# Dynamic convolution and two MoE layers: the first ten cells in an order written out by hand, with the weight units in pairs one cell ahead

## The chip, the core and the metric

The kernel runs on one NeuronCore of a Trainium2 chip. The metric is the device time of one execution in microseconds (us), the median of several runs. The engines are TensorE (PE in the views; its weight loads are PEld), VectorE (DVE), ScalarE (ACT), GpSimd (POOL) and SyncE (SP, which here issues nearly all DMAs). Nothing waits for another core.

## What is computed

A dynamic convolution over the sequence (a softmax over seven taps for each token and head, and the weighted sum of the seven last tokens), then two MoE layers that share one shape: 8192 tokens of 192 features, 2048 hidden features.

```python
def _attn_ref(x, weight_gen):
    B, S, D = x.shape                      # 2, 4096, 192
    H, K = (weight_gen.shape[2], weight_gen.shape[3])   # 8, 7
    w = np.exp(weight_gen - np.max(weight_gen, axis=-1, keepdims=True))
    w = w / (np.sum(w, axis=-1, keepdims=True) + 1e-09)
    x_pad = np.concatenate([np.zeros((B, K - 1, D), dtype=np.float32), x], axis=1)
    idx = np.arange(S)[:, None] + np.arange(K)[None, :]
    x_unf = x_pad[:, idx, :].reshape(B, S, K, H, D // H)
    return np.einsum('bshk,bskhg->bshg', w, x_unf).reshape(B, S, D)

def _moe_ref(x, w_in, w_out):              # layer 0
    h = x @ w_in
    g = np.where(h > 0.0, h, np.exp(np.minimum(h, 0.0)) - 1.0)
    return g @ w_out

def _moe2_ref(x, w_in, w_out):             # layer 1
    h = x @ w_in
    return (h * np.clip(h + 3.0, 0.0, 6.0) / 6.0) @ w_out
```

All of it is float32.

## The kernel before

**Tiling.** The 8192 tokens are 16 blocks of 512. A block goes through a layer in eight *cells*, one for each 256 hidden features, so there are 16 x 2 x 8 = 256 cells, numbered n; the first eight are block 0 in layer 0. The main loop runs over n. In cell n TensorE makes the first product of cell n (x times w_in, into two PSUM banks `h`, one for each half k of the features, from the list `hset`, whose pair alternates with n) and the second product of cell n-3 (g times w_out, summed over the eight cells of a block in the banks `acca` and `accb`; LAG is 3). Both use only 64 of the 128 rows at a time, so matmuls go in pairs, one of each half. Cells 0 to 2 have no second product.

**Precision.** Each float32 operand is split in a high and a low part (`xh`, `xl`; `wi_h`, `wi_l`; `gh`, `gl`), and a product is three: high times high, low times high, high times low. `first_product` lists nine matmuls for each half: "hl1", say, is the high part of w with the low part of x for piece 1.

**A cell's other work.** `act_a` (ScalarE, two passes L520, L521 for each half) and `gate` (VectorE, L537) make r, the activation of h; `round_g` (ScalarE, L527) casts r to gh; `rest_g` (VectorE, L531) makes gl.

**Weight units.** The weights of layer 0 are split on the chip while the first cells run: sixteen units, i0 to i7 (a cell's part of w_in) and o0 to o7 (w_out). A unit goes through: the raw load by DMA (`load_w`; four raw buffers, RAWS; three DMAs for an i unit and one for an o unit); `begin`, an Abs on ScalarE (L147); s0, s1, s2 on VectorE (L151, L154, L158); the cast of the high part on ScalarE (L168); s3, s4 on VectorE (L166, L175); `p5`, three matmuls on TensorE (L180 to L182); and `p6`, the cast of the low part on ScalarE (L187). Before, the groups are [i0], [i1 o0], [i2 o1] and so on, and group n+1 gets its p5 behind the matmuls of cell n, in the banks `aux` and `acca` (and `accb` once), and its p6 behind that cell's activations. A `Stream` deals out the other steps at the end of each cell by due times.

**Queues.** From cell 2 on a DMA that is asked for goes to the list `waiting`, and `transfers` issues a few whenever a half's last matmul in `accb` is done (`told`); up to cell 7 that is two DMAs for the first half and three for the second.

**Block 0's input.** Its convolution is done by VectorE and GpSimd, two tokens of each four. `prepare(0, 0)` transposes it on TensorE into the banks of hset[0], ScalarE casts xh (L328), VectorE subtracts for xl (L330), and then each half of the partitions needs the other's rows as well: four DMAs on SP (two for xh, two for xl), 64x768 each. `Stream`, `round_g`, `rest_g` and `wst.run` set where each step stands in its engine's queue, since every engine works in program order.

Of the kernel before, what the change touches and what calls it, by code (L numbers as in the profile page):

```python
# [17 lines left out]
def kernel(  # L18
# [67 lines left out]
    boot = cpool.tile([P, NF * 2 * D], F32R, tag="wo1", name="boot")  # L86
    w_in = [w.bitcast(U32) for w in (w_in1, w_in2)]
# [25 lines left out]
    class Unit:  # L113


        def __init__(self, kind, m, q):
            self.kind, self.m, self.q = kind, m, q
            self.raw = load_w(kind, m, q)
            self.hw, self.lw = self.raw[:, :, 1], self.raw[:, :, 0]

# [11 lines left out]

        def begin(self):

            bank = aux
            if self.m == 0:

                bank = ((aux, accb), (acca[1], acca[0]))[self.kind == "o"][self.n == 2]
            self.b = bank[:, 0:UN].bitcast(U32)
            if self.m == 0:  # L140
                self.ps = bank[:, 0:UN]
                self.f = fts[self.n][:, self.u * UN:(self.u + 1) * UN].bitcast(U32)
                if self.n > 3:
# [17 lines left out]
        def s3(self):  # L161
            if self.m == 0 and self.n < 4:
                self.r = self.b
            else:
                self.r = stage.tile([P, UN], U32, tag="tr", name="tr", bufs=2)
            nc.vector.tensor_scalar(self.r, self.f, 0xFF800000, None, op0=ALU.bitwise_and)  # L166
            hi, _, v = self.parts()
            nc.scalar.copy(hi, v(self.f.bitcast(F32)))  # L168

        def s4(self):  # L170
            f = o = self.r.bitcast(F32)
            if self.m == 0:
# [51 lines left out]
    def attention(i):  # L224
# [26 lines left out]
        if i == 0:  # L251

            pw = hset[1][0][:, 0:hn * K].rearrange("p (a k) -> p a k", k=K)
            po = hset[0][0][:, 0:2 * D].rearrange("p (t e) -> p t e", e=D)
            hs = [(nc.vector, slice(0, 2), pw, po), (nc.gpsimd, slice(2, 4), w3[:, hn:, :], tmp[:, 0:2])]
        else:
            hs = [(nc.gpsimd, slice(0, TM), w3, tmp)]
# [9 lines left out]
        def product(k):  # L267
            def s():
                for eng, t, w, o in hs:
# [10 lines left out]
        def add():  # L280
            for eng, t, _, o in hs:
                eng.tensor_tensor(y[:, t, :], y[:, t, :], o, op=ALU.add)
# [18 lines left out]
        for k in range(K - 2, -1, -1):  # L301
            steps += [product(k)] + ([add] if k else [add_a, add_d])
# [6 lines left out]
    def prepare(m, i):  # L309
# [26 lines left out]
    def fold_b(m, i):  # L336
# [6 lines left out]
        nc.scalar.copy(b, accb)  # L343
# [70 lines left out]

    def first_product(n, k):
# [7 lines left out]
        for j, (w, x, s) in enumerate((  # L423
                "hh0", "hl0", "lh0", "hh1", "hl1", "lh1", "hh2", "hl2", "lh2")):
# [12 lines left out]
    def second_product(n, k, bank):  # L437
# [4 lines left out]
        acc, p, W = (acca[order.index((m, i)) % 2], accb)[bank], half[k], WO[m]  # L442
        ops = []
        for g in gg[n]:
            for c in range(2):
                for e in ([P] if bank else [0, D + HP] if g is gg[n][0] else [0]):
                    ops.append([acc, W[p, 2 * q + c, e:e + P], g[p, c], False, False, None, None])

# [7 lines left out]
    def whole_second_product(n):  # L456
# [4 lines left out]
        for bank, acc in enumerate((accb, acca[order.index((m, i)) % 2])):  # L461
# [11 lines left out]
    def matmuls(n):  # L473
# [17 lines left out]
        plan = [  # L491
            (s + j, k, op)
            for k, runs in enumerate((
                [(0, b0), (4, a0), (10, l0)], [(0, l1), (7, b1), (11, x1), (13, a1)]))
            for s, ops in runs for j, op in enumerate(ops)]
        seen = [added.pop(i) for i in range(3, NB) if n == prep[0, i] - 1]
        for _, k, (o, w, r, st, sp, wait, tell) in sorted(plan, key=lambda e: e[:2]):
# [5 lines left out]
            if tell:  # L503
# [55 lines left out]
    def later(n, out, in_):  # L559

        if now is None or now >= len(cells) or now < 2 and n == 0:
# [33 lines left out]
    units = [(k, 0, q - (k == "o")) for q in range(NQ + 1) for k in "io" if 0 <= q - (k == "o") < NQ]  # L595
    groups = [units[:1]] + [units[n:n + 2] for n in range(1, len(units), 2)]
    wtasks = [[0, n - 2, len(g)] for n, g in enumerate(groups)]
    for n in range(2 * NQ):
        c = NQ * (n + 2) if n < NB - 2 else start2 + (NQ if n % 2 else 0)
        groups.append([("io"[n % 2], 1, n // 2)])  # L600
        wtasks.append([c - 3 - 2 * (n == NB - 1), c + (3 if n < NB - 1 else 0), 1])
    made, fts = {}, {}

    def want(n):
        if n < len(groups) and n not in made:
            made[n] = [Unit(*u) for u in groups[n]]
            for u, unit in enumerate(made[n]):
                unit.n, unit.u = n, u

    def w_steps(n):  # L610
        def step(k, u):
            def s():
                if k < 0:
                    if u == 0:
                        want(n)
                        want(n + 1)
                        if groups[n][0][1] == 0:

                            fts[n] = act.tile([P, XN], F32, tag="z", name="f", bufs=2)
                    made[n][u].begin()  # L620
                else:
                    getattr(made[n][u], f"s{k}")()
            return s
        return [step(k, u) for k in range(-1, WS if groups[n][0][1] else 5) for u in range(len(groups[n]))]

    wtasks = [
        [b, d, ((WS if groups[n][0][1] else 5) + 1) * c, (lambda n: lambda: w_steps(n))(n)] for n, (b, d, c) in enumerate(wtasks) if n > 1]
    begin = {i: max(7, prep[0, i - 1]) for i in range(2, NB)}
    loads = {max(0, begin[i] - 8): i for i in begin}
# [3 lines left out]
    with tc.manual_schedule():  # L633
        nc.vector.memset(three, 3.0)
        nc.scalar.activation(warm, three, AF.Exp)
        blk[0] = load_block(0, lambda: want(0))
# [4 lines left out]
        blk[1] = load_block(1)  # L641

        todo = {"w": w_steps(0), "a": attention(0)}
        for k in "aaaawwawawawaw":
            todo[k].pop(0)()
        for s in todo["a"] + todo["w"]:
            s()
        made[0][0].p5()
        made[0][0].p6()
# [95 lines left out]
```

## Time and profile before

| | us |
|---|---|
| median of 3 runs | 1226.46 (1225.88 to 1227.32) |
| the profiled execution's own time | 1225.81 |
| its span in the trace | 1224.0 |
| PE busy | 1191.2 (97%) |
| DVE busy | 934.0 (76%) |
| ACT busy | 854.5 (70%) |
| POOL busy | 419.7 (34%) |
| chain that ended last, on PE | 92% |

The span is what the trace covers; 1.8 us of the profiled execution lie around it. The page cuts the span into 40 slices of 30.6 us, so that the ten cells this case is about (22 to about 104 us) are slices 1 to 4. Those are read from the time lines of each engine, which list every instruction with its start, its duration, and in brackets how long the engine had been idle and for whom.

### The profile page before, as it was taken

The page shows a single profiled execution, that of the slowest core. Times are in us where ns is not written, and L with a number is a line of the kernel's source. Part 1 is how long each engine was busy: PE and PEld are TensorE (multiplying, and loading weights), DVE is VectorE, ACT ScalarE, POOL GpSimd, SP SyncE. Part 2 cuts the span into 40 slices and gives each one's busy share as a digit, 9 for nine tenths or more (in the row PEclk, how much of TensorE's full clock was granted, in tenths as well). Part 3 has the DMA queues.
Part 4 walks back from the last instruction along what each step waited for, and adds up shares of the span by engine and source line. Part 5 has one row for each costly group of instructions (what it writes and reads, how often), then busy time and mean ns, then how long its engine had stood idle before and what let it go on. Part 6 is the DMA issues. An engine that isn't in the chain of part 4 may idle for free.

```text
span 1224.0 us, 25360 instructions
## 1 busy us (share of the span) xinstructions
PE 1191.2 (97%) x10146; PEld 948.3 (77%) x10146; DVE 934.0 (76%) x1222; ACT 854.5 (70%) x1337; POOL 419.7 (34%) x235
## 2 busy tenths in 40 slices
PE   3899999999999999999999999999999999999998
PEld 2568778777778777778788888888888888888887
DVE  6778999999999999998777666666666666666664
ACT  2677788888888888888886656556665555666554
POOL 8428778777778877777000000000000000000000
PEclk9899999999999999999999999999999999999999
DMA  6431122221122222111211111111101111110110
GB/s 175 126 115 62 28 88 89 89 89 61 42 76 88 89 89 72 48 59 52 61 57 52 33 34 52 52 40 53 50 23 47 53 53 40 53 36 30 53 40 27
DMA packets 33574, 75.81 MB, mean 62 GB/s; under 512 B 4404, under 2 KB 17074, under 8 KB 33456
## 3 DMA queue, kind: packets, MB, share of 16 engines
q1 hardware_dynamic: 33312, 74.00, 20.9%
q8 instruction: 80, 1.31, 0.5%
q14 instruction: 38, 0.31, 0.1%
q10 hardware_dynamic: 144, 0.20, 0.0%
HBM read 36.43 MB, written 12.58 MB: 40 GB/s over the span
## 4 chain that ended last, share of the span: by engine, by line
PE 92%; DVE 3%; ACT 3%; issue 1%; POOL 1%; DMA 0%; DVEq 0%; POOLq 0%
PE h L498 42%; PE acca L498 28%; PE accb L498 19%; DVE gl L531 1%; ACT gh L527 1%; ACT r L520 0%; PE acca L318 0%; ACT r L521 0%; PE acca L400 0%; DVE r L537 0%; DVE f L158 0%; PE acca L465 0%; ACT f L147 0%; ACT wi_h L168 0%; PE accb L465 0%
## 5 line engine op out<-in xcount | busy, mean ns | idle before, releaser
L498 PE MATMUL h<-xh,wi_l 64*128 64x512 f32 x1536 | 573.1, 397 | 3.5 <-ACT wi_l L187 3.5
L498 PE MATMUL h<-xh,wi_h 64*128 64x512 f32 x1536 | 567.5, 396 | 3.2 <-DVE xl L330 2.6
L498 PE MATMUL h<-xl,wi_h 64*128 64x512 f32 x1536 | 565.0, 395 | 0.8 <-DMA xl<-xl 0.8
L498 PE MATMUL acca<-gh,wo 64*128 64x512 f32 x2024 | 554.8, 393 | 0.0
L531 DVE TENSOR_TENSOR gl<-r,gh 128x1024 fp32r<-128x1024 f32 x256 | 395.5, 1545 | 62.2 <-ACT gh L527 61.2
L498 PEld LDWEIGHTS acca<-gh,wo 64*128 64x128 f32 x2024 | 374.1, 185 | 45.9
L523 ACT ACTIVATE r<-h,three 128x512 f32<-128x512 f32 x256 | 176.1, 688 | 222.5 <-PE h L498 113.2
L498 PE MATMUL accb<-gh,wo 64*128 64x512 f32 x1012 | 320.4, 396 | 0.0
L498 PE MATMUL accb<-gl,wo 64*128 64x512 f32 x1012 | 317.8, 393 | 0.3 <-DVE gl L531 0.3
L498 PE MATMUL acca<-gl,wo 64*128 64x512 f32 x1012 | 317.5, 393 | 0.0
L498 PEld LDWEIGHTS h<-xh,wi_l 64*128 64x128 f32 x1536 | 285.2, 186 | 40.4 <-ACT wi_l L187 5.3
L498 PEld LDWEIGHTS h<-xh,wi_h 64*128 64x128 f32 x1536 | 285.1, 186 | 39.7 <-DVE xl L330 2.8
L498 PEld LDWEIGHTS h<-xl,wi_h 64*128 64x128 f32 x1536 | 284.8, 186 | 36.6 <-DMA xl<-xl 1.4
L540 DVE SCALAR_TENSOR_TENSOR r<-r,h 128x512 f32<-128x512 f32 x256 | 175.9, 687 | 161.0 <-ACT r L523 160.2
L527 ACT CAST gh<-r 128x1024 fp32r<-128x1024 f32 x256 | 266.8, 1042 | 13.4 <-DVE r L537 12.6
L498 PEld LDWEIGHTS acca<-gl,wo 64*128 64x128 f32 x1012 | 187.2, 185 | 23.6
L498 PEld LDWEIGHTS accb<-gl,wo 64*128 64x128 f32 x1012 | 187.0, 185 | 23.6 <-DVE gl L531 0.8
L537 DVE SCALAR_TENSOR_TENSOR r<-r,h 128x512 f32<-128x512 f32 x256 | 172.8, 676 | 39.2 <-ACT r L521 37.8
L498 PEld LDWEIGHTS accb<-gh,wo 64*128 64x128 f32 x1012 | 184.8, 185 | 21.7 <-issue 1.3
L275 POOL TENSOR_TENSOR tmp<-xt,wt 128x768 f32<-128x768 f32 (+1 forms) x96 | 191.0, 1989 | 6.3
L520 ACT ACTIVATE r<-h 128x512 f32<-128x512 f32 x256 | 152.3, 595 | 48.2 <-PE acca L498 28.7
L521 ACT ACTIVATE r<-r 128x512 f32<-128x512 f32 x256 | 162.0, 633 | 8.1
(137 smaller groups left out, 751.5 us busy)
## 6 DMA issues: line engine op xcount, KB each, us to landing
xt<-in_x_dram SPq DMA_DIRECT2D x14, 960.0 KB, 6.0
xh<-xh SPq DMA_DIRECT2D x64, 192.0 KB, 2.7
xl<-xl SPq DMA_DIRECT2D x64, 192.0 KB, 2.8
raw<-in_moe_w_out_dram SPq DMA_DIRECT2D x16, 384.0 KB, 3.3
z<-z SPq DMA_DIRECT2D x16, 384.0 KB, 2.3
zin<-z SPq DMA_DIRECT2D x16, 384.0 KB, 3.0
out_dram<-ot SPq DMA_DIRECT2D x15, 384.0 KB, 4.4
raw<-in_moe_w_in_dram SPq DMA_DIRECT2D x16, 192.0 KB, 3.5
```

Source lines behind the costliest of these rows:

```text
L275: eng.tensor_tensor(o.rearrange("p t (h g) -> p t h g", g=G), xk, wk.rearrange("p (t h) g -> p t h g", h=H), op=ALU.mult)
L498: mm = nc.tensor.matmul(o, w, r, start=st, stop=sp).ins
L520: nc.scalar.activation(r, h, AF.Relu, scale=-1.0)
L521: nc.scalar.activation(r, r, AF.Exp, scale=-1.0)
L523: nc.scalar.activation(r, h, AF.Relu, bias=three)
L527: nc.scalar.copy(gg[n][0], rs[n])
L531: nc.vector.tensor_tensor(gl, rs.pop(n), gh.bitcast(F32), op=ALU.subtract)
L537: nc.vector.scalar_tensor_tensor(r, r, -1.0, h, op0=ALU.add, op1=ALU.max)
L540: nc.vector.scalar_tensor_tensor(r, r, 6.0, h, op0=ALU.min, op1=ALU.mult)
```

## The change

Five things, all of them in the program's first ten cells; from cell 10 on the loop runs as before.

1. The units are handled in the order i0 i1 i2 i3 o0 i4 o1 i5 o2 i6 o3 i7 o4 o5 o6 o7. `turn` says which units' Abs, VectorE steps and high cast stand in cell n, `close` which units' p5 and p6. So the i units run a cell further ahead, o units a cell later, and the last three are alone in cells 7, 8 and 9.
2. `scripts` gives for each cell the order in which the steps are written: M the matmuls, R and G `round_g` and `rest_g` of the cell before, 0 to 4 the units' VectorE steps, H the high casts, x and X `act_a` and `gate` of half 1, y and Y those of half 0, P p5, L p6, J block preparation, B the Abs of the next cell's units. p5 goes, from cell 2 on, to the pair of `hset` that the next cell's first product will write.
3. In the first eight cells the plan of matmuls is another: high parts of x (in cell 0) or of w (in cells 1 to 7) come first in the first product, and the second product's `accb` part stands at slots 6 to 9 and 15 to 18 of 19.
4. Block 0's exchange of rows is done by two ScalarE copies (xh) and two VectorE copies (xl) in place of four DMAs, and its transposes go to `acca`.
5. One of GpSimd's products for block 0 (k = 4) is done by VectorE, in the buffer called `spare`. The softmax of block 2 is a cell later, and so is its load (cell 2).

```diff
     def prepare(m, i):
@@
+            if m == 0 and i == 0:
+                for a in range(2):
+                    nc.scalar.copy(X["h"][half[1 - a], 1], X["h"][half[a], 0].bitcast(F32))
             for src, w in parts:
                 nc.vector.tensor_tensor(w(X["l"]), src, w(X["h"]).bitcast(F32), op=ALU.subtract)
+            if m == 0 and i == 0:
+                for a in range(2):
+                    nc.vector.tensor_copy(X["l"][half[1 - a], 1], X["l"][half[a], 0].bitcast(F32))
+                return
...
     def first_product(n, k):
@@
+        if n < EARLY:
+            kinds = sorted(kinds, key=lambda t: t[n == 0] == "l")
...
     def matmuls(n):
@@
         if n < EARLY:
-            l1, x1 = l1[:7], l1[7:]
+            x1 = first_product(n + 1, 1)[:2] if n == EARLY - 1 else []
+            rows = [(0, a0), (6, b0), (10 if n >= LAG else 0, l0)], [(0, l1), (9, a1), (15, b1), (19, x1)]
         else:
-            l1, x1 = l1[2:], first_product(n + 1, 1)[:2]
-        if n == EARLY - 1:
-            x1 = x1 + first_product(n + 1, 1)[:2]
+            x1 = first_product(n + 1, 1)[:2]
+            rows = [(0, b0), (4, a0), (10, l0)], [(0, l1[2:]), (7, b1), (11, x1), (13, a1)]
@@
-                if now >= 2 and tell[1] == 1:
+                if now > 2 and tell[1] == 1:
                     transfers(1 + k + (now < NQ))
-        if now < 2:
+        if now < 3:
             transfers(len(waiting))
...
-    units = [(k, 0, q - (k == "o")) for q in range(NQ + 1) for k in "io" if 0 <= q - (k == "o") < NQ]
-    groups = [units[:1]] + [units[n:n + 2] for n in range(1, len(units), 2)]
-    wtasks = [[0, n - 2, len(g)] for n, g in enumerate(groups)]
+    BOOT = 10
+    units = [(u[0], 0, int(u[1]), k) for k, u in enumerate("i0 i1 i2 i3 o0 i4 o1 i5 o2 i6 o3 i7 o4 o5 o6 o7".split())]
+    turn = [[1, 2], [3, 4], [5, 6], [7, 8], [9, 10], [11, 12], [13], [14], [15], []]
+    ends = {k: n for n, ks in enumerate(turn) for k in ks} | {0: -1}
+    close = [[1], [2]] + turn[1:-1]
+    boards = [(aux, accb), acca, (aux, acca[1]), (aux, acca[1]), (None, None), (None, None)] + 4 * [(aux,)]
+    scripts = ["M012H34xXyYPLB", "MPR01xX2LyYH34GB", "MR01xX2yYH34GPLB"] + (BOOT - 3) * ["MR012H34GxXJByYPL"]
...
+            if n < BOOT:
+                for k in range(len(made), len(units)):
+                    if ends[k - RAWS] < n:
+                        make(k)
...
-            matmuls(n)
-            if n < NQ:
-                for u in made[n + 1]:
-                    u.p5()
-            if 1 <= n < NQ:
-                round_g(n - 1)
+            if n < BOOT:
+                new, old = [made[k] for k in turn[n]], [made[k] for k in close[n]]
+                spare = hset[(n + 1) % 2][::-1][-len(old):] if n > 1 else [(aux, accb)[n]]
+                work = {
+                    "M": lambda: matmuls(n),
...
+                    "B": lambda: start(n + 1) if n + 1 < BOOT else None}
+                for step in scripts[n]:
+                    work[step]()
```

What the tables make of two engines' queues is shown by the built programs. First ScalarE, around the activations of one cell. `h_73` and `h_72` are the banks of half 1 and half 0 of an even cell's first product, `h_75` and `h_74` those of an odd cell's; `f` and `tr` hold a unit between its steps. Before, cell 3:

```order
51 L168 CAST wi_h<-f 128x384
52 L168 CAST wo_89<-f 128x2x192
53 L527 CAST gh<-r 128x1024
54 L520 ACTIVATE r<-h_75 128x512
55 L521 ACTIVATE r<-r 128x512
56 L520 ACTIVATE r<-h_74 128x512
57 L521 ACTIVATE r<-r 128x512
58 L187 CAST wi_l<-aux 128x384
59 L187 CAST wo_89<-acca_77 128x2x128
60 L187 CAST wo_89<-acca_77 128x2x64
61 L147 ACTIVATE f<-raw 128x384 x2
```

After, cell 4:

```order
56 L544 CAST gh<-r 128x1024
57 L169 CAST wi_h<-f 128x384
58 L169 CAST wo_89<-f 128x2x192
59 L537 ACTIVATE r<-h_73 128x512
60 L538 ACTIVATE r<-r 128x512
61 L147 ACTIVATE tr<-raw 128x384 x2
62 L537 ACTIVATE r<-h_72 128x512
63 L538 ACTIVATE r<-r 128x512
64 L187 CAST wi_l<-h_75 128x384
65 L187 CAST wo_89<-h_74 128x2x128
66 L187 CAST wo_89<-h_74 128x2x64
```

The two Abs (L147) moved from behind p6, the cell's last step, to the place between the two halves' activations, so that half 0's activation and p6 stand behind them; p6 reads banks of `hset`.

TensorE from the last matmuls of cell 3 into cell 4 (`aux`, `acca_77`, `h_73`, `h_72` in L180 to L182 are where p5 writes). Before:

```order
124 L498 MATMUL h_74<-xh,wi_l 128x512
125 L498 MATMUL acca_76<-gl,wo_89 128x512
126 L180 MATMUL aux<-f,ident 128x384
127 L181 MATMUL aux<-wi_h,minus 128x384
128 L182 MATMUL aux<-boot,plus 128x384
129 L180 MATMUL acca_77<-f,ident 128x384
130 L181 MATMUL acca_77<-wo_89,minus 128x384
131 L182 MATMUL acca_77<-boot,plus 128x384
132 L498 MATMUL accb<-gh,wo_89 128x512
133 L498 MATMUL h_73<-xh,wi_h 128x512
```

After:

```order
118 L515 MATMUL h_74<-xh,wi_l 128x512
119 L515 MATMUL accb<-gl,wo_89 128x512
120 L180 MATMUL h_73<-f,ident 128x384
121 L181 MATMUL h_73<-wi_h,minus 128x384
122 L182 MATMUL h_73<-boot,plus 128x384
123 L180 MATMUL h_72<-f,ident 128x384
124 L181 MATMUL h_72<-wo_89,minus 128x384
125 L182 MATMUL h_72<-boot,plus 128x384
126 L515 MATMUL acca_76<-gh,wo_89 128x512
127 L515 MATMUL h_73<-xh,wi_h 128x512
```

The cell's last matmul is now the one into `accb` that lets `transfers` issue, and p5 writes the two banks that cell 4's own first product writes next (its second instruction).

## Rows read from the trace of the kernel before

**Rows 1.** The page: span; busy us, share, instructions; granted clock by 40 slices.

```profile
span 1224.0 us, 25360 instructions
PE 1191.2 (97%) x10146; PEld 948.3 (77%) x10146; DVE 934.0 (76%) x1222; ACT 854.5 (70%) x1337; POOL 419.7 (34%) x235
PEclk9899999999999999999999999999999999999999
```

**Rows 2.** Windows: length, busy of PE, PEld, DVE, ACT, POOL; granted clock; DMA share, GB/s.

```profile
22.57:33.41 10.84, 10.03 (x26) 6.43 (x26) 5.95 (x12) 3.91 (x7) 10.45 (x7) 1.00 0.75 208
40.25:50.48 10.23, 7.09 (x22) 4.93 (x21) 8.28 (x20) 7.17 (x15) 4.08 (x4) 0.50 0.83 240
50.49:60.00 9.51, 9.51 (x56) 6.52 (x55) 8.23 (x18) 7.98 (x16) 0.00 (x0) 1.00 0.38 108
```

**Rows 3.** Time line of PE: start, duration, instruction, [idle before, its releaser].

```profile
29.03 0.62 PE L498 MATMUL h<-xh,wi_l 64*128 64x512 f32 x1
33.62 0.49 PE L498 MATMUL h<-xh,wi_h 64*128 64x512 f32 x1
39.04 0.91 PE L180 MATMUL accb<-f,ident 128*128 128x384 f32 x2 [2.25 <-DVE boot L175]
46.45 0.79 PE L498 MATMUL h<-xh,wi_l 64*128 64x512 f32 x1 [3.14 <-ACT wi_l L187]
...
53.09 0.50 PE L498 MATMUL accb<-gh,wo 64*128 64x512 f32 x1
58.00 0.91 PE L180 MATMUL aux<-f,ident 128*128 128x384 f32 x2
60.19 0.50 PE L498 MATMUL accb<-gh,wo 64*128 64x512 f32 x1
...
94.82 0.39 PE L498 MATMUL accb<-gh,wo 64*128 64x512 f32 x1
99.28 0.40 PE L498 MATMUL accb<-gh,wo 64*128 64x512 f32 x1
```

**Rows 4.** Time line of DVE, the same columns.

```profile
21.50 1.01 DVE L330 TENSOR_TENSOR xl<-h,xh 128x384 fp32r<-128x384 f32 x2
34.73 0.57 DVE L151 TENSOR_SCALAR accb<-accb 128x384 f32<-128x384 f32 x1 [3.06 <-ACT accb L147]
39.38 0.56 DVE L151 TENSOR_SCALAR aux<-aux 128x384 f32<-128x384 f32 x1
44.92 0.69 DVE L537 SCALAR_TENSOR_TENSOR r<-r,h 128x512 f32<-128x512 f32 x1 [0.83 <-ACT r L521]
81.04 1.22 DVE L531 TENSOR_TENSOR gl<-r,gh 128x1024 fp32r<-128x1024 f32 x1
84.57 2.33 DVE L531 TENSOR_TENSOR gl<-r,gh 128x1024 fp32r<-128x1024 f32 x1
```

**Rows 5.** Time line of ACT, the same columns.

```profile
20.04 0.84 ACT L328 CAST xh<-h 128x384 fp32r<-128x384 f32 x2
41.81 0.51 ACT L168 CAST wi_h<-f 128x384 fp32r<-128x384 f32 x1 [2.80 <-DVE f L158]
42.69 1.04 ACT L527 CAST gh<-r 128x1024 fp32r<-128x1024 f32 x1
59.52 0.58 ACT L520 ACTIVATE r<-h 128x512 f32<-128x512 f32 x1
60.67 0.46 ACT L187 CAST wi_l<-aux 128x384 fp32r<-128x384 f32 x1
```

**Rows 6.** Time line of SP (issues), then the page's DMA issues with median us to landing.

```profile
54.52 2.28 SPq L571 DMA_DIRECT2D raw<-in_moe_w_in_dram  x3
56.91 0.51 SPq L571 DMA_DIRECT2D raw<-in_moe_w_out_dram  x1
...
raw<-in_moe_w_out_dram SPq DMA_DIRECT2D x16, 384.0 KB, 3.3
```

**Rows 7.** Time line of POOL, the same columns.

```profile
21.80 1.54 POOL L275 TENSOR_TENSOR y<-xt,wt 128x768 f32<-128x768 f32 x1 [2.76 <-issue]
```

More of the change, by code (lines that the diff above doesn't have):

```diff
@@ L86 @@
     boot = cpool.tile([P, NF * 2 * D], F32R, tag="wo1", name="boot")
+    fts = [act.tile([P, XN], F32, tag="z", name="f", bufs=2) for _ in range(2)]
     w_in = [w.bitcast(U32) for w in (w_in1, w_in2)]
@@ L265, in s2, with product @@
                 v.tensor_tensor(w3, w3, s.to_broadcast(shp), op=ALU.mult)
-        def product(k):
+        def product(k, ahead=None):
             def s():
-                for eng, t, w, o in hs:
+                for eng, t, w, o in ahead or hs:
+                    if i == 0 and k == AHEAD and not ahead and eng is nc.gpsimd:
+                        continue
                     nt = t.stop - t.start
@@ L301, in attention @@
         for k in range(K - 2, -1, -1):
-            steps += [product(k)] + ([add] if k else [add_a, add_d])
+            steps += [product(k)] + ([(lambda k: lambda: add(k))(k)] if k else [add_a, add_d])
+        if i == 0:
+            steps.append(product(AHEAD, [(nc.vector, slice(2, 4), w3[:, hn:, :], spare)]))
         return steps
@@ L411, in give, with accs @@
         return evict
+    def accs(m, i):
+        return acca[order.index((m, i)) % 2], accb
     def first_product(n, k):
@@ L441, in second_product @@
         m, i, q = cells[n]
-        acc, p, W = (acca[order.index((m, i)) % 2], accb)[bank], half[k], WO[m]
+        acc, p, W = accs(m, i)[bank], half[k], WO[m]
         ops = []
@@ L447, in second_product @@
                     ops.append([acc, W[p, 2 * q + c, e:e + P], g[p, c], False, False, None, None])
+        if not bank and n + LAG < EARLY:
+            ops = ops[0::2][:2] + ops[4:] + ops[1:4:2]
         ops[0][3] = q == 0 and k == 0
@@ L460, in whole_second_product @@
         ops = []
-        for bank, acc in enumerate((accb, acca[order.index((m, i)) % 2])):
+        for bank, acc in enumerate((accb, accs(m, i)[0])):
             ws = [(g, c, e) for g in (gh, gl) for c in range(2)
@@ L559, in later @@
     def later(n, out, in_):
-        if now is None or now >= len(cells) or now < 2 and n == 0:
+        if now is None or now >= len(cells) or now < 3 and n == 0:
             nc.sync.dma_start(out, in_)
@@ L601 @@
-        wtasks.append([c - 3 - 2 * (n == NB - 1), c + (3 if n < NB - 1 else 0), 1])
-    made, fts = {}, {}
+        wtasks.append([c - 3 - 2 * (n == NB - 1), c + (3 if n < NB - 1 else 0), WS + 1, (lambda n: lambda: w_steps(n))(n)])
+    second = {}
     def want(n):
[L605 to L608, printed above, removed]
+        if n < len(groups) and n not in second:
+            second[n] = Unit(*groups[n])
@@ L610, in w_steps @@
     def w_steps(n):
[L611 to L624, printed above, removed]
@@ L626, with begin @@
-    wtasks = [
-        [b, d, ((WS if groups[n][0][1] else 5) + 1) * c, (lambda n: lambda: w_steps(n))(n)] for n, (b, d, c) in enumerate(wtasks) if n > 1]
+        def begin():
+            want(n)
+            want(n + 1)
+            second[n].begin()
+        return [begin] + [(lambda k: lambda: getattr(second[n], f"s{k}")())(k) for k in range(WS)]
     begin = {i: max(7, prep[0, i - 1]) for i in range(2, NB)}
-    loads = {max(0, begin[i] - 8): i for i in begin}
+    loads = {max(2, begin[i] - 8): i for i in begin}
@@ L641, with start @@
         blk[1] = load_block(1)
[L643 to L646, printed above, removed]
-            s()
-        made[0][0].p5()
-        made[0][0].p6()
+        for k in (1, 2, 3):
+            make(k)
+        def start(n):
+            for k, bank in zip(turn[n], boards[n]):
+                made[k].masks(bank)
+        u, c0 = made[0], attention(0)
+        ahead = c0.pop()
+        for s in c0[:5]:
+            s()
+        u.masks(aux)
+        for s in (u.s0, u.s1, u.s2, u.high, u.s3, u.s4, ahead):
+            s()
+        u.p5(aux)
+        u.p6()
+        for s in c0[5:]:
+            s()
         c1 = attention(1)
@@ L653 @@
         prepare(0, 0)()
-        for s in c1[4:] + w_steps(1):
+        start(0)
+        for s in c1[4:]:
             s()
```

138 lines of the change are left out of this document (72 added, 66 removed).

## The prediction

> **What bounds the kernel now.** I read the page first: PE is busy 97% of the span, so nearly all of the run is TensorE's own work, and the change leaves every matmul in place. What can be won is PE's idle time and slow time [rows 1]. The granted clock by slices is 9, 8 and then 9 throughout, so the slow stretch lies in the first 60 us. The windows put it there: the clock stands at 0.50 (the lower level, 1.2 of 2.4 GHz) from 40.25 to 50.48 and at 1.00 behind that [rows 2]. PE's time line gives the marks [rows 3]. I call the matmuls of cell n mm(n). mm(0) ends at 29.65; mm(1) starts at 33.62; PE then idles 2.25 us for a unit's s4 and 3.14 us for a p6; mm(3), the first cell with both products, starts at 53.09; mm(4) at 60.19, mm(9) at 94.82, mm(10) at 99.28. A cell without a unit's p5 costs 99.28 - 94.82 = 4.46 us; cell 3 with the p5 pair 7.10, the pair itself 60.19 - 58.00 = 2.2. All 256 cells follow the same loop from cell 10 on in both kernels, so the question is one number: when does mm(10) start?
>
> **To mm(3): ten us won.** I walk the changed queues with these durations.
>
> - Cell 0. xh's casts start at 20.04 and take 0.84 as a pair [rows 5]; I put them at 20.15, since VectorE's extra product makes GpSimd's chain about 0.1 later at its end. High parts come first, so mm(0) starts at 21.1 on the half that needs no exchange. The exchange copies on ScalarE (64x768) are not in the trace: between a 384-wide cast, 0.51, and the 1024-wide one, 1.04 [rows 5]; I take 0.8 each by width, done at 22.7. The same on VectorE: the subtractions take 1.0 [rows 4], the copies lie between 0.5 (a step of a unit) and 2.33 (the gl subtraction that takes 1.22 alone, when GpSimd runs beside it); I take 0.5, because a copy reads one operand as a unit's step does. xl is whole at about 23.2. A pair of matmuls takes 4.46 / 19 = 0.235 at full pace; mm(0) has nine and runs now at the slow pace (0.62 for a matmul in place of 0.40, [rows 3]): 4.2, and 0.6 of waits for the copies, so it ends at 25.9, 3.75 earlier than now.
> - Unit pair i1, i2: ten VectorE steps take 39.38 - 34.73 = 4.65 [rows 4], so about 23.2 to 27.8; p5 of i1 ends at 28.0. mm(1), nine pairs, follows from 28.0 to 31.5 (now from 33.62); I let its pace rise on the way, as it now does within two products.
> - Pair i3, o0: s0 and s1 behind the gates of cell 0 (29.6); each gate 0.69 [rows 4] waits for its activation (two passes, 1.2) [rows 5]; the second gate of cell 1 ends at 35.06, and s3, s4 of the pair (four steps, 1.85) at 36.9.
> - ScalarE then holds the path: the Abs of o1 shares o0's bank and waits for its s4 (0.55, to 37.45), gh(1) 0.95 (38.4), four passes of cell 2 (40.75), the two high casts, which wait for s2 (42.5), p6 of i3 0.46 [rows 5]. mm(3) starts at 42.95 in place of 53.09: **10.1 won.**
>
> **From mm(3) to mm(10): thirteen lost.** Now 99.28 - 53.09 = 46.2 [rows 3]. After, three things add up.
>
> 1. *PE's own work.* Seven cells of 4.46 are 31.2; four p5 pairs at 2.2 and three single p5 at 1.1 are 12.1 (now four pairs and one single, since the first four groups are through before mm(3)); block 1's transposes and two extra matmuls 1.3. Sum 44.6.
> 2. *A new wait.* The Abs of the next pair stands on ScalarE between half 1's and half 0's activation, and the raw tile's last parts are let out by the cell's last matmul into `accb`, which is now the cell's last matmul of all. So from mm(n)'s end: 0.1 to the issue, 0.6 for the i unit's third part (three take 2.28, [rows 6]), then 3.4 from the o unit's issue to its landing (the page's median is 3.3, [rows 6]), Abs 0.5, half 0's two passes 1.15, p6 0.46: 6.2. Behind the Abs on ScalarE stand that activation and p6; PE waits for p6, because p5 now writes the banks of the next cell's first product. PE itself needs 2.2 of the 6.2 for p5, so it idles 4.0 us between mm(3) and mm(4) and, with part of the chain under way, 3.1 more than in a plain cell between mm(4) and mm(5). Cell 5 to 6 has 2.2 (block 1's xl and o5's Abs stand ahead of half 0). Cells 6 to 9 wait 0.05, 0.54, 0.7 and 0.6, mostly for p6 of o5, o6, o7, which are alone there. Sum 11.2.
> 3. *The clock.* Now, PE stands idle 2.25 us, does a p5, and at 40.25 the clock falls; after the 3.14 us of idle it is still at 0.50 and rises at 50.49 [rows 2, 3]. After the change PE idles about 5.1 us ahead of mm(3) and 4.0 ahead of mm(4), both longer than either. So I expect two falls. Of the one in the trace, 46.45 to 50.48 is steady work at half speed: 4.0 us that do 2.0 us of work. I take 1.9 for each fall; its bounds are 0 (no fall) and 3.5 (half of the 7.09 busy us of the whole slow stretch, [rows 2]). Sum 3.8.
>
> That makes 44.6 + 11.2 + 3.8 = 59.6, mm(10) at 102.55. Against 46.2 that is 13.4 lost, and **13.4 - 10.1 = 3.3 us slower.** From the profiled execution's 1225.81 this is 1229.1; the median stands 0.65 above that execution, so 1226.46 + 3.3 = **1229.8.**
>
> The other edits come out at nothing. Block 2's softmax a cell later moves GpSimd's work on block 2 by a part of a cell, and block 2 enters only at cell 13. Where GpSimd slows the gl subtraction now (2.33 for 1.22, [rows 4]) it does so after as well. Block 2's load still leaves several cells ahead of its use.
>
> On the new wait a rule of the Trainium skill bears, "DMA: Bandwidth & Descriptors", section "Rules for kernel authors": issue a DMA early, compute, and wait for it late. The change waits early, in the middle of the cell, for a DMA issued at the end of the same cell's matmuls. By the trace's rows that is the 4.0 and 3.1 us above; were the wait behind p6, as now, they would go and the sum would stand near -4 in place of +3.3.
>
> **Rivals.**
>
> *The clock stays up.* The record shows 1.00 through PE's 2.25 us of idle, and the fall only 3.8 us after mm(1)'s end. If the p5 group and short idle times keep it up at mm(3) and mm(4), the 3.8 go: mm(10) at 98.8, 0.5 faster than now, 1226.0. It decides at the first matmuls of mm(3): 0.62 long at the low level, 0.40 at the high one. Against it: both idle times are longer than now. Chance 0.23.
>
> *Full pace from the first product on* (the other side). From 22.57 to 33.41 the clock's record reads 1.00, but matmuls last 0.62 as at the low level [rows 2, 3]. If after the change they run at full pace from mm(0), p5 of i1 takes 0.9 in place of 1.6 and mm(1), nine pairs, 2.1 in place of 3.5 to 4: the chain of gates, s4, Abs and activations moves 2.7 up, mm(3) starts near 40.2, its idle time is shorter, and the two falls don't come. 3.3 - 2.7 - 3.8 = -3.2: 1223.3, and up to 3 less if the chains on ScalarE have slack that I left out. For it: mm(0) has fewer gaps. Against: PE has the same 2 us of idle ahead of it, and the slow pace begins right there now. Chance 0.20.
>
> *More is lost.* VectorE's two copies run while GpSimd begins block 1 (its first product lies at 21.80, 1.54 long, [rows 7]). If each waits for one such instruction, 3.1 us go on top in front of all unit steps: +6.4, 1232.9. A third slow stretch, at mm(5), or falls that last as long as the one now, cost 1.7 to 3.2: up to 1233 as well. Together chance 0.15, reaching to 1235.
>
> Of VectorE and GpSimd the Trainium skill ("SBUF — State Buffer", section "Who interferes with whom") says that only the port pair they share is contended, as a lock held for a whole instruction. The subtraction's step from 1.22 to 2.33 beside GpSimd agrees; by the rule the copies would wait as in this rival, by the plain row they take 0.5.
>
> **How the numbers follow.** Forecast 0.42: 1227.9 to 1232. Clock up 0.23, full pace 0.20, more lost 0.15. A difference of 0.2%, 2.45 us, is about what a measurement of this kernel can tell from none. Faster by more: the full-pace case and 0.05 of the clock's, 0.25. Within: 0.18 of the clock's and 0.05 of the forecast's low end, 0.23. Slower: 0.37 + 0.15 = 0.52. Both signs hold much, so the likeliest case's own range is given above; the range for 8 in 10 runs from 1221 (the lower part of the full-pace case) to 1235.
>
> **What would show it.** mm(3) should start near 43 (41 to 45), with an idle of about 5 us ahead of it that ends on ScalarE's p6. The Abs (L147) of cells 3 and 4 should show an idle before it that ends on a raw DMA; PE should idle about 4 and 3 us ahead of mm(4) and mm(5), released by ScalarE's p6. The window from mm(3) to mm(5) should hold two stretches at 0.50. mm(10), the first `accb` row of that cell, should lie near 102.5, 3.3 later than now. I am wrong if the raw tiles land before ScalarE asks for them (then cells 3 and 4 last under 9 us), if mm(3) comes much before 41 or behind 45, or if the clock shows no fall behind 40 us.

## The result and the profile after

The changed kernel takes 1240.18 us (median of 4 runs, 1237.81 to 1242.55) against 1226.89 (4 runs of before beside them): ratio 1.0108, 95% interval 1.0081 to 1.0136. It is slower, 13.3 us, as forecast in sign; but 3.3 had been forecast, and the range ended at 1235.

The page after, the lines that answer to [rows 1]:

```profile
span 1236.0 us, 25367 instructions
PE 1191.7 (96%) x10146; PEld 946.1 (77%) x10146; DVE 938.8 (76%) x1225; ACT 856.7 (69%) x1339; POOL 416.8 (34%) x234
PEclk9899999999999999999999999999999999999999
```

PE's busy time is the same but for 0.5 us, so 11.5 of the 12 us of span are time in which it stands. Its time line after, the lines with an idle in the ten cells (and mm(10), the last), against [rows 3]:

```profile
29.16 1.65 PE L180 MATMUL aux<-f,ident 128*128 128x384 f32 x2 [3.06 <-DVE boot L174]
46.08 0.79 PE L515 MATMUL h<-xh,wi_h 64*128 64x512 f32 x1 [4.99 <-ACT wi_l L187]
58.20 0.50 PE L515 MATMUL h<-xh,wi_h 64*128 64x512 f32 x1 [3.29 <-ACT wi_l L187]
70.41 0.79 PE L515 MATMUL h<-xh,wi_h 64*128 64x512 f32 x1 [2.97 <-ACT wi_l L187]
79.95 0.50 PE L515 MATMUL h<-xh,wi_h 64*128 64x512 f32 x1 [0.92 <-ACT wi_l L187]
97.40 0.79 PE L515 MATMUL accb<-gh,wo 64*128 64x512 f32 x1 [4.24 <-ACT wo L187]
105.38 0.49 PE L515 MATMUL accb<-gh,wo 64*128 64x512 f32 x1 [0.63 <-ACT wo L187]
111.92 0.49 PE L515 MATMUL accb<-gh,wo 64*128 64x512 f32 x1 [0.63 <-ACT wo L187]
```

These are mm(3) to mm(6), mm(8), mm(9) and mm(10) (the second matmul of a cell up to mm(6), the first from mm(8) on). mm(10) starts at 111.92, against 99.28 before: 12.64 later. From there to the end it is 1236.0 - 111.92 = 1124.1 us, before 1224.0 - 99.28 = 1124.7. So the whole loss lies ahead of mm(10), as forecast, and 9.4 us of it were not in the sum (102.55).

Windows over the matmuls of cells 3, 4, 5, 6 and 8 (columns as in [rows 2]):

```profile
46.08:52.29 6.21, 6.21 (x38) 4.69 (x38) 6.21 (x13) 3.61 (x8) 0.00 (x0) 0.73 0.33 123
58.20:64.44 6.24, 6.24 (x38) 4.77 (x38) 6.14 (x15) 3.50 (x7) 0.00 (x0) 0.73 0.17 53
70.41:76.42 6.01, 6.01 (x38) 4.62 (x38) 5.94 (x14) 4.57 (x10) 0.00 (x0) 0.76 0.14 29
79.95:84.66 4.71, 4.71 (x38) 3.65 (x38) 4.45 (x10) 3.12 (x7) 0.00 (x0) 1.00 0.21 48
97.40:103.56 6.16, 6.16 (x39) 4.75 (x39) 6.02 (x8) 2.79 (x4) 5.92 (x4) 0.74 0.01 3
```

Cell 6 starts behind 0.92 us of idle, at 1.00, and takes 4.71; the four cells behind idle times of 2.97 to 4.99 us run a part of their matmuls at the lower level (cell 4 only from 59.5 on) and lose 1.50, 1.53, 1.30 and 1.45: 5.8 us.

ScalarE after, the Abs of cells 3, 4 and 7:

```profile
54.72 0.55 ACT L147 ACTIVATE tr<-raw 128x384 f32<-128x384 f32 x1 [1.54 <-DMA raw<-in_moe_w_in_dram]
56.09 0.54 ACT L147 ACTIVATE tr<-raw 128x384 f32<-128x384 f32 x1 [0.83 <-DMA raw<-in_moe_w_out_dram]
66.94 0.54 ACT L147 ACTIVATE tr<-raw 128x384 f32<-128x384 f32 x1 [3.93 <-DMA raw<-in_moe_w_in_dram]
68.30 0.54 ACT L147 ACTIVATE tr<-raw 128x384 f32<-128x384 f32 x1 [0.81 <-DMA raw<-in_moe_w_out_dram]
95.22 0.52 ACT L147 ACTIVATE aux<-raw 128x384 f32<-128x384 f32 x1 [4.66 <-DMA raw<-in_moe_w_out_dram]
```

The wait for the loads is where the prediction put it in cells 3 and 4, and once more in cell 7 (o7's load), where it had none. The transfer of o7's load on SP, behind a load of one of the token blocks:

```profile
89.48 0.34 SPq L588 DMA_DIRECT2D xt<-in_x_dram  x1
89.88 0.42 SPq L588 DMA_DIRECT2D raw<-in_moe_w_out_dram  x1
```

VectorE and GpSimd at the exchange of rows, after:

```profile
21.00 1.02 DVE L339 TENSOR_TENSOR xl<-acca,xh 128x384 fp32r<-128x384 f32 x2 [0.20 <-ACT xh L334]
22.06 2.74 DVE L342 CAST xl<-xl 64x768 fp32r<-64x768 f32 x2
21.02 1.54 POOL L279 TENSOR_TENSOR y<-xt,wt 128x768 f32<-128x768 f32 x1 [1.09 <-PE acca L327]
22.53 1.86 POOL L279 TENSOR_TENSOR tmp<-xt,wt 128x768 f32<-128x768 f32 x1
```

The two copies take 2.74 us (0.92 and 1.81), not 1.0, while GpSimd's products run beside them. Each ends about 0.4 us behind the end of the product beside it: 22.98 behind 22.56, and 24.80 behind 24.39.

### The profile page after: what moved, and what is told of

Read it like the earlier page. It is cut to its first block, busy times and chain, and to the rows that moved or that the text cites. A ratio compares the mean times of both kernels' runs of the same rounds, so it can differ in the third digit from the quotient of the medians.

```text
span 1236.0 us, 25367 instructions
## 1 busy us (share of the span) xinstructions
PE 1191.7 (96%) x10146; PEld 946.1 (77%) x10146; DVE 938.8 (76%) x1225; ACT 856.7 (69%) x1339; POOL 416.8 (34%) x234
## 4 chain that ended last, share of the span: by engine, by line
PE 92%; DVE 4%; DMA 2%; ACT 2%; issue 0%; SPq 0%; DVEq 0%; ACTq 0%
PE h L515 42%; PE acca L515 28%; PE accb L515 19%; DMA raw<-in_moe_w_out_dram 1%; DVE gl L548 1%; PE acca L327 1%; DMA xt<-in_x_dram 1%; DVE r L554 1%; ACT r L538 0%; PE acca L413 0%; ACT r L537 0%; PE acca L485 0%; DVE h L279 0%; DVE f L158 0%; PE accb L485 0%
## 5 line engine op out<-in xcount | busy, mean ns | idle before, releaser
L515 PE MATMUL h<-xh,wi_h 64*128 64x512 f32 x1536 | 566.7, 397 | 13.6 <-ACT wi_l L187 12.2
L515 PE MATMUL acca<-gh,wo 64*128 64x512 f32 x2024 | 560.5, 395 | 0.0
```

Of the source, the lines that this page charges most:

```text
L515: mm = nc.tensor.matmul(o, w, r, start=st, stop=sp).ins
```

## The experiments

All are edits of the changed kernel unless it says otherwise; ratios are against the kernel before on the same chip. Three suspects: the load that ScalarE waits for in mid-cell, the copies beside GpSimd, and the clock.

**1. Which half of the wait is the cause: where the Abs stands, or when the load leaves?**

```diff
- "MR012H34GxXJByYPL"     # cells 3 to 9
+ "MR012H34GxXJyYPLB"
```

> Edit: from cell 3 on the Abs of the next cell's units stands at the end of the cell on ScalarE, behind half 0's activation and p6, as in the kernel before. Loads leave as late as in the changed kernel. Theory A (the place of the Abs is the cause): PE no longer idles ahead of mm(4), mm(5), mm(6) and mm(8); the cells take 8.2 and then about 6.9 us, 16 us less by mm(10), about 1224. Theory B (the late issue of the loads is the cause, the Abs only the place where it shows): half 0's activation and p6 get free, but the loads still land 4.6 us after a cell's last matmul and the ten VectorE steps follow, so p5 of the next cell waits for s4 in every second cell (periods about 7 and 9.4): some 11 us less by mm(10), about 1229, with PE idle now put down to VectorE's boot (s4).

```diff
  # load_w, layer 0: at the top of the cell in place of the list
- later(0, dst, src)
+ nc.sync.dma_start(dst, src)
```

> Edit: layer 0's raw loads are issued by SP at the top of the cell, ahead of the cell's matmuls, and not from the list that the accb matmuls let out; the Abs stays between the two activations. Theory A (the place of the Abs): little changes as long as the Abs is there; less than 4 us. Theory B (the late issue): the raw tiles are there when ScalarE asks, no idle of ScalarE before L147 ends on a DMA in cells 3 to 8, cells 3 to 7 take 8.2 and then about 6.9 us in place of 12.1, 12.2, 9.5, 6.9, 10.6, the three later falls of the clock go with the idle time: 16 us less, about 1224.

Measured: the first 1224.76 us, ratio 0.9989 (0.9980 to 0.9999); the second 1225.05, 0.9994 (0.9985 to 1.0004). Each by itself gives back about 15 us. In the first, mm(3) to mm(10) takes 100.19 - 48.76 = 51.4 us; in the second 98.56 - 46.19 = 52.4; in the changed kernel 111.92 - 46.08 = 65.8. PE's idle time behind mm(3) is gone in both but for 0.6 to 1.1 us ahead of mm(8), mm(9) and mm(10) and these lines, both mm(6) (first kernel, then second):

```profile
72.81 0.50 PE L515 MATMUL h<-xh,wi_h 64*128 64x512 f32 x1 [0.30 <-ACT wi_l L187]
```

```profile
71.64 0.49 PE L517 MATMUL h<-xh,wi_h 64*128 64x512 f32 x1 [1.27 <-ACT wi_l L189]
```

So neither theory alone: the stop needs both, an early Abs and a late load. (mm(3) itself comes at 48.76 in the first kernel and at 46.08 in the changed one, though nothing ahead of it was edited: mainly, the first product starts 0.4 later, and i1's p5 and mm(1) run at the slow pace throughout, 30.26 to 36.68, 6.4 us, where the changed kernel took 29.16 to 34.18, 5.0.) The second kernel agrees with the Trainium skill's rule named in the prediction ("DMA: Bandwidth & Descriptors", "Rules for kernel authors"); the first shows that moving the wait behind the work that others need does as much here.

**2. Do VectorE's copies wait for GpSimd?** The step that lets GpSimd start is moved behind them.

```diff
- for s in c1[:4]: s()
+ for s in c1[:3]: s()
  prepare(0, 0)()
+ c1[3]()
  start(0)
```

> Edit: the last softmax step of block 1 on VectorE (L267), which lets GpSimd start on block 1, stands behind the two exchange copies in place of ahead of the subtractions. Nothing else moves. Theory A (the copies wait for GpSimd): the pair of copies takes about 1.0 in place of 2.74 us, the chain to mm(3) is 1.3 to 1.7 earlier, 1.5 us less in all, 1238.7. Theory B (a copy across partition halves is that slow by itself): the copies stay near 2.7, mm(3) stays at 46.1 or comes 0.4 later by the moved step, no change.

Measured: 1237.65 us, ratio 1.0090 (1.0068 to 1.0111). VectorE, GpSimd and PE in this kernel:

```profile
22.11 1.12 DVE L342 CAST xl<-xl 64x768 fp32r<-64x768 f32 x2
23.88 1.55 POOL L279 TENSOR_TENSOR y<-xt,wt 128x768 f32<-128x768 f32 x1 [3.90 <-issue]
28.01 0.91 PE L180 MATMUL aux<-f,ident 128*128 128x384 f32 x2 [1.49 <-DVE boot L174]
42.99 0.79 PE L515 MATMUL h<-xh,wi_h 64*128 64x512 f32 x1 [4.51 <-ACT wi_l L187]
```

The copies take 1.12 in place of 2.74; theory A. mm(3) starts at 42.99, where the prediction had 42.95. The copies by themselves are not all of the 3.1 us that mm(3) gains: counted from the first product (21.46 here, 21.41 in the changed kernel), i1's p5 starts 1.2 earlier; that p5 and mm(1) take 3.56 (28.01 to 31.57) in place of 5.02, 1.5 less, since they run at full pace here; and the gl subtraction in cell 2, beside GpSimd in both, takes 1.68 in place of 2.17, 0.5 less. Yet the median falls by only 2.5 us, the intervals of the two ratios overlap, and mm(10) comes at 111.78 in place of 111.92. The gain went to the clock, cells 3, 4, 5 and 8 of this kernel:

```profile
42.99:49.71 6.72, 6.72 (x38) 5.10 (x38) 6.72 (x13) 3.18 (x7) 5.20 (x4) 0.67 0.38 144
55.55:62.77 7.22, 7.21 (x38) 5.50 (x38) 6.21 (x15) 3.59 (x7) 0.00 (x0) 0.62 0.15 45
68.70:76.14 7.44, 7.44 (x38) 5.66 (x38) 6.54 (x15) 4.57 (x10) 0.00 (x0) 0.59 0.26 76
95.97:103.42 7.45, 7.45 (x39) 5.65 (x39) 4.78 (x8) 2.79 (x4) 7.21 (x4) 0.59 0.01 2
```

The same cells behind idle times of the same length take 28.8 us here and 24.6 above: a fall cost 1.3 to 1.5 us there and 2.0 to 2.7 here. That is not the edit's doing as far as the runs show: of this kernel's four executions, three have a mean granted clock of 0.989 and take 1237.59 to 1239.14, and one has 0.993 and takes 1233.65.

**3. The exchange of xl by DMA again.**

```diff
- nc.vector.tensor_copy(X["l"][half[1 - a], 1], X["l"][half[a], 0].bitcast(F32))
+ nc.sync.dma_start(X["l"][half[1 - a], 1].bitcast(F32), X["l"][half[a], 0].bitcast(F32))
```

> Edit: xl's rows are exchanged by two DMAs on SP again, xh's by ScalarE copies as changed; high parts still come first. If VectorE's queue is what sets mm(3) (theory A), its unit steps start 2.7 earlier, mm(0) ends within 1 us of now since xl is needed for its last three pairs only, and mm(3) starts 2 to 2.7 earlier: about 1237.8. If ScalarE's and PE's queues set it (theory B), mm(3) stays within 0.5 us: no change. If the DMAs land behind the loads queued on SP ahead of them, mm(0) ends later by some us and the time is longer.

Measured: 1239.54 us, ratio 1.0115 (1.0100 to 1.0130), no change against the changed kernel. Counted from the first product, the first pair of units is ready 1.2 us earlier, but mm(0) ends 5.9 in place of 4.7 us after its start (it waits for the DMA), mm(1) runs 30.79 to 35.00 at the slow pace, and mm(3) starts 24.8 after the first product (changed kernel 24.7). What VectorE won, PE's slower mm(1) took: 4.2 us, against 2.8 in the changed kernel. Experiment 1's first kernel shows the same 4.2 (32.48 to 36.68) without this edit, so whether the slow mm(1) belongs to the edit, and which theory holds, stays open.

**4. What the falls of the clock cost.** Extra matmuls fill PE's idle time.

```diff
+ if step == "P":                       # behind p5 of cells 2, 3, 4, 5, 7
+     ...                               # rhs: high part of block 0, one half
+     for _ in range({2: 18, 3: 12, 4: 11, 5: 4, 7: 17}.get(n, 0)):
+         nc.tensor.matmul(accb if n == 2 else acca[1], WI[0]["h"][half[0], 0:P], rhs, start=True, stop=True)
```

> Edit: the changed kernel with extra matmuls (high parts of block 0, results never used) behind p5 of cells 2, 3, 4, 5 and 7, in a bank that is free there: 18, 12, 11, 4 and 17 of them, about as long as PE's idle time at these places. The waits for the loads stay. Theory A (the falls of the clock are a cost of their own, 1.5 to 3 us each, and their length differs from run to run): the matmuls of cells 3, 4, 5 and 8 take about 4.7 in place of 6.2 us each, some 6 us less than the changed kernel and up to 10 less than its slow runs, 1231 to 1234, with a smaller spread. Theory B (the slow matmuls only fill time that the next raw load would cost anyway): mm(10) stays near 112, no change.

Measured: 1235.55 us (1233.09 to 1236.67), ratio 1.0074 (1.0059 to 1.0090): 4.6 less than the changed kernel. From mm(3) on the granted clock stays at 1.00, mm(4) takes 61.40 - 56.69 = 4.71, and mm(10) starts at 107.18, 4.7 earlier. The time lies 1.5 above the band that theory A gave. Its page and one filled idle:

```profile
PEclk9999999999999999999999999999999999999999
53.15 3.08 PE L715 MATMUL acca<-xh,wi_h 64*128 64x512 f32 x12 [0.39 <-DVE boot L174]
```

So the falls are a cost of their own: filling the idle time gives back about a third of the 13.3. The waits are the larger part: mm(3) to mm(10) still takes 107.18 - 45.85 = 61.3 us, against 46.2 before.

**5. The late load in cell 7.** A first try hit the wrong unit.

```diff
+ if kind == "o" and m == 0 and q == 6:      # then q == 7
+     nc.sync.dma_start(raw..., w_out...)    # at the top of the cell
```

> Edit: the changed kernel, and only o6's load is issued at the top of cell 7, ahead of the block load that now stands before it in the list. Theory A (the late issue of that one load costs cell 8): ScalarE's idle of 4.7 us ahead of o6's Abs and PE's of 4.2 ahead of mm(8) go, and the slow clock in mm(8) with them: 4.2 + 1.5 = 5.7 less, about 1234.5. Theory B (the block load of 960 KB keeps the DMA rings busy, whichever is first): the Abs still waits some 3 us, and less than 2 us are won.

Measured: 1241.99 us, ratio 1.0122 (1.0107 to 1.0138), from three executions; a fourth took 2368.45 and is left out of both. A miss: the Abs that waits in cell 7 is o7's, not o6's, and it still waited 4.75 us (and o6's load is asked for in cell 5, so that is where the edit issued it). This kernel is of use for the clock all the same: its one edit moves a load that was not late, and the matmuls of its cells 3, 4, 5 and 8 take 7.10, 7.33, 7.40 and 7.36 us where the changed kernel's profile has 6.21, 6.24, 6.01 and 6.16, 4.6 us more in all. The same edit for o7:

> Edit: the changed kernel, and only o7's load (the Abs that ScalarE waits 4.7 us for in cell 7) is issued at the top of cell 6, ahead of block 1's exchange and the block load that stand before it in the list; the earlier edit of this kind hit o6's, which was not late. Theory A (the place in the list): no idle of ScalarE ahead of that Abs, none of PE ahead of mm(8), and mm(8) at full pace: 4.2 + 1.5 to 3 = 6 to 7 less, 1233 to 1235.5. Theory B (the DMA rings are full then): the Abs still waits, less than 2 us won.

Measured: 1236.03 us, ratio 1.0071 (1.0057 to 1.0085). ScalarE's Abs, and mm(8) at full clock:

```profile
93.59 0.51 ACT L151 ACTIVATE aux<-raw 128x384 f32<-128x384 f32 x1
96.90:101.62 4.72, 4.72 (x39) 3.67 (x39) 4.55 (x7) 2.65 (x4) 4.56 (x3) 1.00 0.01 3
```

From the start of cell 7 to mm(10) it takes 109.98 - 89.89 = 20.1, in the changed kernel 111.92 - 86.78 = 25.1: 5 us for one load's place in the list, theory A. The whole run gains 4.2, less than the 6 to 7 expected, since the falls in cells 3 to 5 cost 3.3 us more in this execution than in the changed kernel's profile. In the list the load stood behind block 1's four exchange DMAs and a block load of 960 KB; it left with the first of cell 7's two signals, at 89.88, and the Abs that needs it started 5.3 us later.

**6. Mending it.** Loads first, GpSimd later, and in cell 2 p5 and p6 ahead of the activations:

```diff
- "MR01xX2yYH34GPLB"      # cell 2
+ "MPR01LxX2yYH34GB"
```

> Edit: the changed kernel with three mends: layer 0's raw loads leave at the top of the cell (as e2), GpSimd starts block 1 behind VectorE's exchange copies (as e3), and in cell 2 p5 and p6 of i3 and o0 stand behind the first cast of gh in place of behind the activations and the high casts. If the three causes are the ones the traces name: copies 1.1, mm(3) starts near 39 to 40 (43 by e3, 46 by e2), no idle ahead of mm(4) to mm(8), mm(10) near 92 to 94 in place of 98.6 in e2, 5 to 6 us less than e2: about 1219 to 1220, 0.5% under the kernel before. Rival: what is won ahead of mm(3) is given back, because VectorE's steps for the next pair are then late for p5 of cell 3 (PE idle put down to boot, s4): mm(10) near 97, 1223 to 1224.

Measured: 1223.46 us, ratio 0.9972 (0.9962 to 0.9982). mm(3) starts at 40.44, near what was expected, but the rival's sum came true by another cause (mm(10) at 97.61):

```profile
40.44 0.50 PE L517 MATMUL h<-xh,wi_h 64*128 64x512 f32 x1 [0.49 <-ACT wi_l L189]
48.57 0.79 PE L517 MATMUL acca<-gh,wo 64*128 64x512 f32 x1 [5.76 <-SPq L523]
45.92 1.91 SPq L98 DMA_DIRECT2D raw<-in_moe_w_in_dram  x3
```

A load at the top of cell 3 waits on SP for a raw buffer (3.1 us, for the s4 that reads it last), and then takes 2.5 us to issue with the one behind it; the signal by which one half's product lets the other's into the same bank stands behind both on SP. So loads of cell 3 go back to the list, with the Abs of that cell last; or, in another kernel, all Abs go last and the loads stay late:

> Edit: the three mends of e6 with one difference: the loads of cell 3 leave through the list as in the changed kernel (at the top they kept SP in cell 3 waiting for raw buffers, and the signals between the halves' products stood behind them on SP: 5.8 us of PE), and in cell 3 alone the Abs stands at the end of the cell. If the list was right about that: mm(3) runs from 40.4 without the stop, p5 of cell 3 waits some 2 us for s4, mm(4) near 50, p5 of cell 4 one more wait, then cells of 6.9 and 6.5: mm(10) near 90.5, 7 less than e6, about 1217. Rival: what comes earlier at mm(3) is lost again to VectorE's steps in cells 3 to 5 (PE idle put down to boot, s4), mm(10) at 95 to 97, 1221 to 1223.

> Edit: e1 (the Abs at the end of the cell from cell 3 on, loads as late as in the changed kernel) with GpSimd's start behind the copies (e3) and the early p5 and p6 of cell 2 (e6). e1 took 51.4 from mm(3) to mm(10). Theory A (nothing of the chain ahead of mm(3) is needed again later): mm(3) at 40.5 and 51.4 later mm(10), 92, 8 less than e1, 1217. Theory B (in e1 VectorE had time for the next units while PE stood ahead of mm(3)): mm(4) and mm(5) wait for s4, at least half of it is lost, 1220 to 1222.

Measured: 1224.31 us, 0.9975 (0.9965 to 0.9986), and 1223.97, 0.9978 (0.9969 to 0.9987). Both rivals: the time won ahead of mm(3) is lost again at mm(4), 5.7 and 6.3 us, but to ScalarE's p6, not to s4:

```profile
55.30 0.79 PE L517 MATMUL h<-xh,wi_h 64*128 64x512 f32 x1 [5.73 <-ACT wi_l L189]
```

There p6 of i4 (54.79) stood behind two high casts, which waited 1.96 for VectorE's s2, and four passes:

```profile
51.60 0.51 ACT L171 CAST wi_h<-f 128x384 fp32r<-128x384 f32 x1 [1.96 <-DVE f L160]
```

So p5 goes right behind the matmuls and p6 ahead of the activations in every cell; s2 to s4, the high casts and gl come behind half 1's activation:

```diff
- "MR012H34GxXJByYPL"     # cells 3 to 9
+ "MPR01LxXJ2yYH34GB"
```

> Edit: the changed kernel with GpSimd's start behind the copies, and in every cell from 2 to 9 p5 right behind the matmuls and p6 right behind the cast of gh, ahead of both activations; the Abs of the next units at the end of the cell; loads late as in the changed kernel. In e9 and e10 PE stood 5.7 and 6.3 us ahead of mm(4), because p6 of i4 stood on ScalarE behind two high casts and four passes. If that order is what is left: mm(4) comes near 50 (55.3 in e9), a pair of units then costs VectorE ten steps, gl and two gates, 4.65 + 1.2 + 1.4 = 7.3 a cell, mm(10) near 90 to 92: 1217 to 1219. Rival: half 1's activation, now behind p6, holds up the gates and so s2 to s4 of the next pair, and PE waits for s4 (boot) in every pair cell: mm(10) near 97, 1223.

> Edit: e11, and in cells 3 to 9 the first signal of the accb matmuls lets out four DMAs in place of two, so a pair's loads leave 2 us earlier, in the middle of the cell. If the late landing is on the path in e11 (ScalarE idle ahead of the Abs, ended by a raw DMA), 1 to 2 us a pair cell are won, 3 to 6 in all. If not (VectorE's steps set the pace), no change against e11, or a little worse if SP waits there for raw buffers and holds up the signals.

Measured: **1218.11 us, ratio 0.9930 (0.9916 to 0.9944)**, and 1218.15, 0.9928 (0.9913 to 0.9943). The first of them in the ten cells:

```profile
41.04 0.49 PE L515 MATMUL h<-xh,wi_h 64*128 64x512 f32 x1 [0.49 <-ACT wi_l L187]
48.94 0.49 PE L515 MATMUL h<-xh,wi_h 64*128 64x512 f32 x1 [0.45 <-ACT wi_l L187]
PEclk9999999999999999999999999999999999999999
```

mm(10) starts at 90.80, 8.5 ahead of the kernel before, and from mm(3) on the clock stays up. Loads 2 us earlier add nothing (the edit lets both of a cell's signals issue four DMAs): mm(3) to mm(10) takes 50.0 with them and 49.8 without, so in this order the late loads are off the path, as the second theory said. So with other places for a few steps in three queues the change is 0.7% faster than the kernel before, in place of 1.1% slower. Which of its five parts brings the gain was not tried apart.

## Why the prediction was right and where it was wrong

The sign and the place were right, the size was not: 13.3 us slower where 3.3 were forecast, beyond the range's end at 1235. Three terms of the sum were too small: the VectorE copies ahead of mm(3), the wait ahead of mm(8), and the number of falls of the clock.

- *What bounds the kernel, and where to look:* right. All of the difference lies between the first product and mm(10).
- *To mm(3), 10.1 won:* 7.0 (53.09 to 46.08), 3.1 short. The term that failed is the price of VectorE's copies: 0.5 each, "because a copy reads one operand as a unit's step does", and 0.92 and 1.81 in the run. The copy was put beside a step of a unit, which reads or writes PSUM there and keeps its 0.55 beside GpSimd in the changed kernel too; the row of the gl subtraction beside GpSimd, 2.33 for 1.22 [rows 4], was the nearer one, since it, too, moves SBUF data only. The Trainium skill's rule ("SBUF — State Buffer", "Who interferes with whom") agrees: 0.56 us alone, 0.92 and 1.81 beside GpSimd. The rival "more is lost" had this cause, but that its 3.1 us is the loss measured is luck: the copies take 1.7 us more than was put, and the rest came by way of the slower p5 and mm(1) and the gl subtraction (experiment 2).
- *The walk to mm(3) with the copies at their price:* 42.99 in experiment 2, where the prediction had 42.95. From mm(1)'s end on it holds within about 0.1 us; ahead of that two errors cancel, since i1's p5 ends at 29.2 and not 28.0, and mm(1) then takes 2.4 us at full pace and not 3.5.
- *The new wait, cells 3 to 5:* right in place and cause, and near in size for the first two. mm(3) to mm(4) takes 12.1 (the terms give 4.46 + 2.2 + 4.0 + 1.9 = 12.6), mm(4) to mm(5) 12.2 (11.7, and block 1's transposes on top); ScalarE's Abs waits for a raw DMA and PE for p6. mm(5) to mm(6) takes 9.5 (8.9), but by luck: the stop behind p5 is 0.8 shorter than put (1.42 in place of 2.2, 78.53 to 79.95), and a fall of 1.3 that had not been put there makes up for it.
- *Cells 6 to 9, "0.05, 0.54, 0.7 and 0.6":* wrong for cell 7, 4.24 in place of 0.54, the largest miss. I had followed which step p6 waits for, but not where o7's load stands in the list of transfers, behind the exchange of block 1 and the block load. That is +3.7 us (experiment 5). The other two, 0.63 and 0.63, were right.
- *The clock, two falls of 1.9:* four falls, 5.8 us in the profiled run. The third (behind 2.97 us of idle) had been named in a rival, the fourth follows from the wait that I missed. +2.0. One reading was off here: mm(1) ends at 36.79 in the kernel before, so the fall came 3.5 us behind it, not 3.8.
- *Sum:* 3.1 + 3.7 + 2.0 is 8.8 of the 9.4 us between 102.55 and 111.92. The other 0.6 is a balance of small terms: a cell takes 4.64 from its restart to the p5 behind it (mm(6), 79.95 to 84.59) and not 4.46, 1.3 in seven cells, against the 0.8 of cell 5 to 6. The rest of the 13.3 is the run: the profiled execution (1237.81) is the fastest of four, whose times reach 1242.55. The clock is the likely reason: the four have a mean granted clock of 0.991, 0.992, 0.989 and 0.988 at 1237.81, 1238.08, 1242.29 and 1242.55, and experiment 5's first kernel, profiled at 1241.99, pays 10.4 us for the same four falls in place of 5.8. The slower executions of the changed kernel itself were not profiled.
- *Rivals:* "The clock stays up" and "full pace from the first product" did not come; the first matmuls of mm(0) and of mm(3) take 0.62 or more. Both halves of "more is lost" came, the copies and the third fall, and its end of 1235 was passed because the wait ahead of mm(8) stood in no rival.
- *"Were the wait behind p6":* the prediction put -4 for that. Experiment 1's first kernel is 1.1 us faster than the kernel before; the loss ahead of mm(3), 3.1 in the changed kernel, stays in it.

## What to carry to other kernels

When a wait for a DMA is put into an engine's queue, two places decide: what stands behind the wait on that engine, and what lets the DMA go; mending either took 15 us off here, the falls of the clock behind the stops included. Follow every transfer through the list it is queued in, up to the last one of the stretch, since the one that was not followed cost 3.7 us of wait and a fall of the clock, more than any other miss. And put a step that frees another engine (here p6) ahead of steps whose results are needed a cell later: in one edit with the steps that had to give way, that turned 1224 into 1218.

## What was not expected of the hardware

- A VectorE copy of 64x768 float32 within SBUF takes 0.56 us alone, and 0.92 and 1.81 us with GpSimd's products running; each of the two ends 0.4 us behind the product beside it.
- The price of a fall of TensorE's clock behind about the same idle (3 to 5 us) differs from execution to execution: 1.3 to 1.5 us in the changed kernel's profile, 2.4 to 2.7 in that of a kernel which differs in one load that was not late, and 2.0 to 2.7 in experiment 2, so that 3.1 us won ahead of them were not seen at the end.
- The granted clock reads 1.00 from 32.48 to 36.68 in experiment 1's first kernel, where a 64x512 matmul takes 0.63 us in place of 0.40: the pace has to be read from the durations there, as in [rows 2] and [rows 3] from 22.57 on.
- A 384 KB load issued 0.4 us behind a 960 KB one let its reader start after 5.3 us; the median to landing is 3.3 [rows 6]. This is one transfer.
- A DMA that waits on SP for its buffer held up a plain signal behind it, and PE with it, for 5.8 us, of which it waited 3.1 for the buffer.
